# Two attention plans shifted by a few groups, and one weight transfer cut in two, in a kernel bound by TensorE

## The chip, the cores and the metric

One core of one Trainium2 chip. The time is that of one execution on the device, in microseconds; lower is better. A kernel is run several times, and medians are quoted.

## The reference, cut to what matters

```python
k_proj = np.einsum('ks,bhsd->bhkd', E, k)          # 8 batches, 8 heads, 1024 tokens, head size 64
v_proj = np.einsum('ks,bhsd->bhkd', F, v)          # 1024 keys and values become 64
attn   = softmax(scale * q @ k_proj.T)             # 1024 x 64 in each head
x      = (attn @ v_proj) as 8192 tokens x 512
h      = x @ w_in                                  # 512 -> 2048
out    = (h * clip(h + 3, 0, 6) / 6) @ w_out       # 2048 -> 512
```

The attention is small beside the two matrix products that follow it, which are nine tenths of the matmul time.

## The kernel before: the parts that the change and the argument touch

The work goes batch by batch. While the main products of batch b run, the attention of batch b+1 is slipped in between their groups of matmuls, so that ScalarE and VectorE do its exponentials, logarithms and products beside TensorE. There are two kinds of main group: 4 matmuls with w_in (0.86 us), and an output group of 16 matmuls with w_out (3.45 us). Every matmul writes a PSUM tile, which another engine then has to read. The tile of a w_in group is read by a relu on ScalarE and by a product on VectorE (the "relu eviction"), that of an output group by a copy, mostly on ScalarE (the "output copy").

```python
ps_mm = tile_pool(name="ps_mm", bufs=4, space=PSUM)   # tiles of the main groups
ps_at = tile_pool(name="ps_at", bufs=4, space=PSUM)   # tiles of the attention
...
def quads(self, stationary, j):
    tiles = [pat() for _ in range(NB)]                # NB = 2; pat() takes a tile of ps_at
    ...                                               # two matmuls into each
def normalised(self, j):
    den = self.quads(lambda r, h: ones[r:r + KP, :D], j)         # sums of exponentials
    av = self.quads(lambda r, h: self.vp[r:r + KP, h, :], j)     # times the values
    lns = [log(den[t]) for t in range(NB)]                       # ScalarE
    yield
    for t in range(NB):
        nc.vector.tensor_mul(self.xT[:, j, t, :], av[t], inverse(lns[t]))   # ScalarE, then VectorE
        yield
```

A plan is a list of (wait, part, argument): let `wait` places go by, then issue the part. Places lie after each w_in group and after each output group (in batch 1's plan, after each quarter of an output group). "two_scores" makes 16 score matmuls into all four attention tiles; ScalarE reads each tile with an exponential. "project" fills one tile with keys and values, which VectorE copies out in "keys_out" and "values_out". In each plan the four "normalised" steps are called the first to the fourth below, and in the prediction "normalised" 1 to 4; their arguments in the code are 0 to 3. Each gives ScalarE two logarithms and two "reciprocals" (exponentials of the negated logarithm), and VectorE two products. The prediction numbers the groups of a half batch from 0. PSUM tiles are handed out by the framework when the kernel is built, so which tile a matmul gets, and thus what it waits for, can be read from the built program.

The softmax here doesn't subtract the row's maximum and nothing guards it: scores larger than these inputs give would overflow.

## Time and profile before

| | |
|---|---|
| median time | 518.07 us (518.07 to 518.13, 3 runs) |
| span of the profiled run | 516.5 us |
| TensorE busy | 502.4 us, 97% |
| next busiest engine, ScalarE | 282.0 us, 55% |

Where TensorE idles is seen best in the view by windows. The columns are the stretch, its length, TensorE's busy time and instructions, its clock, the busy share of the DMA engines and what they moved:

```profile
0.00:20.00 20.00, 16.94 (x144) 1.00 1.15 180
20.00:36.00 16.00, 15.23 (x81) 1.00 1.29 205
66.00:87.00 21.00, 20.26 (x135) 1.00 1.04 186
104.00:137.00 33.00, 30.95 (x184) 1.00 0.90 152
198.00:460.00 262.00, 259.78 (x1398) 1.00 0.40 86
```

Outside the start and the end, three stretches idle: that of the w_in loads (20 to 36), batch 1's attention (66 to 87) and batch 2's (104 to 137). In the 262 us of the later batches it is under 1%.

### The profile page before, as it was taken

The page shows a single profiled execution, that of the slowest core. Times are in us where ns is not written, and L with a number is a line of the kernel's source. Part 1 is how long each engine was busy: PE and PEld are TensorE (multiplying, and loading weights), DVE is VectorE, ACT ScalarE, POOL GpSimd, SP SyncE. Part 2 cuts the span into 40 slices and gives each one's busy share as a digit, 9 for nine tenths or more (in the row PEclk, how much of TensorE's full clock was granted, in tenths as well). Part 3 has the DMA queues.
Part 4 walks back from the last instruction along what each step waited for, and adds up shares of the span by engine and source line. Part 5 has one row for each costly group of instructions (what it writes and reads, how often), then busy time and mean ns, then how long its engine had stood idle before and what let it go on. Part 6 is the DMA issues. An engine that isn't in the chain of part 4 may idle for free.

```text
span 516.5 us, 7173 instructions
## 1 busy us (share of the span) xinstructions
PE 502.4 (97%) x2752; PEld 222.7 (43%) x2802; DVE 239.4 (46%) x377; ACT 282.0 (55%) x517; POOL 37.2 (7%) x56
## 2 busy tenths in 40 slices
PE   8899999999999999999999999999999999999996
PEld 4444444434344444444444444444444444444442
DVE  3573735744455345445444453544535544344420
ACT  3657466575556743766436753566545674444431
POOL 8510020020020000200010000200000000000000
PEclk9999999999999999999999999999999999999999
DMA  9999999499169511984119820397111011001112
GB/s 169 202 204 208 202 162 209 93 155 212 41 103 214 123 43 30 153 175 102 41 52 188 175 67 34 70 205 151 41 42 39 34 42 41 28 35 43 41 43 80
DMA packets 73683, 55.40 MB, mean 107 GB/s; under 512 B 35504, under 2 KB 65456, under 8 KB 73648
## 3 DMA queue, kind: packets, MB, share of 16 engines
q0 software_dynamic: 31424, 29.36, 36.0%
q1 hardware_dynamic: 42000, 25.17, 18.3%
q8 instruction: 22, 0.36, 0.3%
q10 hardware_dynamic: 224, 0.39, 0.3%
q14 instruction: 13, 0.11, 0.1%
HBM read 59.24 MB, written 16.78 MB: 147 GB/s over the span
## 4 chain that ended last, share of the span: by engine, by line
PE 89%; DMA 3%; ACT 2%; issue 2%; DVE 2%; POOL 1%; another core or an unknown queue 0%; DVEq 0%; ACTq 0%; POOLq 0%
PE mm L421 41%; PE mm L401 41%; PE at L224 3%; PE at L181 3%; DMA w_in_sb<-in_moe_w_in_dram 2%; PE at L210 1%; DMA k<-in_k_dram 1%; DVE g L407 1%; ACT ln L158 0%; ACT r L406 0%; POOL q L97 0%; ACT aT L215 0%; POOL k L101 0%; DVE xT L235 0%
## 5 line engine op out<-in xcount | busy, mean ns | idle before, releaser
L407 DVE SCALAR_TENSOR_TENSOR g<-r,mm 128x512 bf16<-128x512 f32 x256 | 173.2, 685 | 207.0 <-ACT r L406 206.7
L401 PE MATMUL mm<-xT,w_in_sb 128*128 128x512 bf16 x1001 | 232.5, 379 | 3.4 <-issue 1.7
L421 PE MATMUL mm<-w_out_sb,g 128*128 128x512 bf16 x997 | 229.4, 379 | 1.3 <-issue 0.2
L406 ACT ACTIVATE r<-mm 128x512 f32<-128x512 f32 x256 | 152.2, 602 | 67.3 <-PE mm L401 65.6
L401 PEld LDWEIGHTS <-w_in_sb 128*128 128x128 bf16 x1024 | 97.0, 98 | 125.5 <-issue 12.8
L421 PEld LDWEIGHTS <-g 128*128 128x128 bf16 x1024 | 98.9, 98 | 120.6 <-issue 3.8
L435 ACT COPY o_sb<-mm 128x512 f32<-128x512 f32 x59 | 34.3, 586 | 140.0 <-PE mm L421 134.9
L235 DVE TENSOR_TENSOR xT<-at,rec 128x512 bf16<-128x512 f32 x56 | 38.0, 684 | 24.8 <-ACT rec L163 24.8
L163 ACT ACTIVATE rec<-ln 128x512 f32<-128x512 f32 x60 | 37.5, 637 | 0.0
L158 ACT ACTIVATE ln<-at 128x512 f32<-128x512 f32 x60 | 33.0, 615 | 6.2 <-PE at L224 3.9
L215 ACT ACTIVATE aT<-at 128x512 bf16<-128x512 f32 x56 | 29.0, 610 | 2.0 <-PE at L210 2.0
L199 POOL COPY mark<-kT 1x1 bf16<-1x1 bf16 x5 | 0.9, 177 | 246.6 <-DMA kT<-kp 246.6
L224 PE MATMUL at<-aT,vp 64*64 64x512 bf16 x112 | 12.7, 378 | 1.3 <-ACT ln L158 0.8
L181 PE MATMUL at<-k,e_t 128*64 128x512 bf16 x56 | 13.4, 382 | 0.0
L181 PE MATMUL at<-v,f_t 128*64 128x512 bf16 x56 | 13.4, 382 | 0.0
L224 PE MATMUL at<-aT,ones 64*64 64x512 bf16 x112 | 11.5, 400 | 0.1
L210 PE MATMUL at<-qT,kT 64*64 64x256 bf16 x224 | 9.1, 275 | 1.0 <-DVE vp L190 0.9
L190 DVE CAST vp<-at 64x512 bf16<-64x512 f32 x14 | 9.7, 694 | 0.3
L187 DVE CAST kp<-at 64x512 bf16<-64x512 f32 x14 | 8.9, 676 | 1.1 <-PE at L181 1.1
L181 PEld LDWEIGHTS <-e_t 128*64 128x64 bf16 x56 | 5.6, 109 | 7.3 <-issue 3.0
L84 PE MATMUL mm<-ones 128*128 128x512 bf16 x18 | 7.0, 521 | 1.5 <-DVE ones L77 1.5
L224 PEld LDWEIGHTS <-ones 64*64 64x64 bf16 x112 | 3.2, 103 | 11.9 <-issue 11.9
(57 smaller groups left out, 109.0 us busy)
## 6 DMA issues: line engine op xcount, KB each, us to landing
out_dram<-o_sb SPq DMA_DIRECT2D x63, 256.0 KB, 2.0
k<-in_k_dram POOLq DMA_DIRECT2D x7, 1024.0 KB, 14.7
v<-in_v_dram POOLq DMA_DIRECT2D x7, 1024.0 KB, 20.1
q<-in_q_dram POOLq DMA_DIRECT2D x7, 1024.0 KB, 9.8
w_out_sb<-in_moe_w_out_dram POOLq DMA_DIRECT2D x4, 512.0 KB, 18.0
w_in_sb<-in_moe_w_in_dram POOLq DMA_DIRECT2D x3, 512.0 KB, 12.4
k<-in_k_dram POOLq DMA_DIRECT2D x4, 256.0 KB, 5.5
v<-in_v_dram POOLq DMA_DIRECT2D x4, 256.0 KB, 7.7
```

The costliest lines, as they stand in the source:

```text
L158: nc.scalar.activation(ln, den, AF.Ln)
L163: nc.scalar.activation(rec, ln, AF.Exp, scale=-1.0)
L181: nc.tensor.matmul(ps[e * KP:(e + 1) * KP], ef_t[e][:, so, :], kqv[self.b]["kv"[e]][:, :, so, :], start=(so == 0), stop=(so == SO - 1))
L210: nc.tensor.matmul(tiles[r][t * KP:(t + 1) * KP, a * HT:(a + 1) * HT], self.kT[r * D:(r + 1) * D, 2 * j + a, :], qT[r * D:(r + 1) * D, j, ...
L215: nc.scalar.activation(self.aT[j][:, r].rearrange("p a n -> p (a n)"), tiles[r], AF.Exp, scale=scale)
L224: nc.tensor.matmul(tiles[t][c:c + D].rearrange("p (r n) -> p r n", r=2), stationary(r, 2 * j + a), self.aT[j][r:r + KP, :, a, :], start=Tr ...
L235: nc.vector.tensor_mul(self.xT[:, j, t, :], av[t], inverse(lns[t]))
L401: nc.tensor.matmul(h_ps, w_in_sb[:, ko, fo * P:(fo + 1) * P], xT[:, ko, t, :], start=(ko == 0), stop=(ko == KO - 1))
L406: nc.scalar.activation(r, h_ps, AF.Relu, bias=0.5, scale=1.0 / 6.0)
L407: nc.vector.scalar_tensor_tensor(g[:, fo, :], r, 1.0, h_ps, op0=ALU.min, op1=ALU.mult)
L421: nc.tensor.matmul(o_ps, g[:, fo, c * P:(c + 1) * P], w_out_sb[:, fo, :], start=(fo == 0), stop=(fo == FO - 1))
L435: (copy or nc.scalar.copy)(o_sb, o_ps)
```

## The change

Its intent: let the first groups start on w_in sooner, and move the attention steps of batches 1 and 2 to places where what they wait for is ready.

```diff
-    for lo, n in ((0, 128), (128, 128), (256, 256), (512, 512), (1024, 512), (1536, 512)):
+    for lo, n in ((0, 128), (128, 128), (256, 256), (512, 256), (768, 256),
+                  (1024, 512), (1536, 512)):
         load_w_in(lo, n)
 ...
     PLANS = {1: (... (2, "values_out", 1),
-                 (1, "two_scores", 0), (3, "two_scores", 2), (1, "normalised", 0),
+                 (1, "two_scores", 0), (2, "two_scores", 2), (2, "normalised", 0),
                  (0, "normalised", 1), (0, "normalised", 2), (0, "normalised", 3)),
              2: ((10, "project"), (0, "keys_out"), (1, "turn"), (2, "values_out", 0), (3, "values_out", 1),
-                 (1, "two_scores", 0), (2, "two_scores", 2), (3, "normalised", 0),
-                 (0, "normalised", 1), (1, "normalised", 2), (0, "normalised", 3))}
+                 (3, "two_scores", 0), (1, "two_scores", 2), (4, "normalised", 0),
+                 (0, "normalised", 1), (0, "normalised", 2), (0, "normalised", 3))}
```

## The prediction

> **What bounds the kernel now.** I read the page of the profile first, for the share of each engine and the chain that ended last; then TensorE's timeline, for every place where it stops; then the timelines of ScalarE and VectorE around those places, to see what TensorE was waiting for.
>
> ```profile
> span 516.5 us, 7173 instructions
> PE 502.4 (97%) x2752; PEld 222.7 (43%) x2802; DVE 239.4 (46%) x377; ACT 282.0 (55%) x517; POOL 37.2 (7%) x56
> ...
> PE 89%; DMA 3%; ACT 2%; issue 2%; DVE 2%; POOL 1%; another core or an unknown queue 0%; DVEq 0%; ACTq 0%; POOLq 0%
> ```
>
> TensorE is the bound: 97% busy, and 89% of the chain is its own matmuls; the next engine is at 55%. The change adds and removes no TensorE instruction (2752 matmuls stand in both), it only moves some. So all it can do is shorten or lengthen the places where TensorE stops, and 516.5 - 502.4 = 14.1 us is the whole idle time, of which the table of windows puts 3.1 into the first 20 us and 4.4 into the last 56.5. The prize is a few tenths of a per cent. I list the stops that the change can reach.
>
> First, the wait for w_in. The columns 512 to 1023 come in one transfer, and the fifth group needs its first 128 columns:
>
> ```profile
> 24.60 9.67 PE L401 MATMUL mm<-xT,w_in_sb 128*128 128x512 bf16 x43 [0.35 <-DMA w_in_sb<-in_moe_w_in_dram]
> ```
>
> Second, batch 1. "normalised" is 4 matmuls with ones and 4 with vp; run freely (77.25 to 77.81) it takes 0.56 us. At 73.18 it takes until 74.79, so 1.61:
>
> ```profile
> 71.65 0.63 PE L210 MATMUL at<-qT,kT 64*64 64x256 bf16 x16
> 72.22 1.04 PE L421 MATMUL mm<-w_out_sb,g 128*128 128x512 bf16 x4
> 73.18 0.47 PE L224 MATMUL at<-aT,ones 64*64 64x512 bf16 x4
> 73.73 0.89 PE L224 MATMUL at<-aT,vp 64*64 64x512 bf16 x4
> 74.79 2.54 PE L421 MATMUL mm<-w_out_sb,g 128*128 128x512 bf16 x11 [0.16 <-issue]
> 77.25 0.41 PE L224 MATMUL at<-aT,ones 64*64 64x512 bf16 x4
> 77.50 0.39 PE L224 MATMUL at<-aT,vp 64*64 64x512 bf16 x4
> 77.81 2.76 PE L421 MATMUL mm<-w_out_sb,g 128*128 128x512 bf16 x12
> ```
>
> ```profile
> 72.11 2.07 ACT L215 ACTIVATE aT<-at 128x512 bf16<-128x512 f32 x4 [1.19 <-PE at L210]
> ```
>
> The attention has four PSUM tiles. The scores just before fill all four, and each is free only when its exponential has read it: ScalarE does that until 74.18, and the last two matmuls with vp need the fourth. The idle mark shows little of this (0.16), since a stretched group counts as busy; the start of the following row shows it. The loss is 1.61 - 0.56 = 1.05 us.
>
> Third, batch 2, with three stops:
>
> ```profile
> 104.25 0.51 PE L210 MATMUL at<-qT,kT 64*64 64x256 bf16 x9
> 105.64 0.41 PE L210 MATMUL at<-qT,kT 64*64 64x256 bf16 x7 [0.88 <-DVE vp L190]
> 105.98 1.90 PE L401 MATMUL mm<-xT,w_in_sb 128*128 128x512 bf16 x8
> ...
> 123.62 0.41 PE L224 MATMUL at<-aT,ones 64*64 64x512 bf16 x4
> 123.86 0.85 PE L224 MATMUL at<-aT,vp 64*64 64x512 bf16 x4
> 124.64 3.63 PE L421 MATMUL mm<-w_out_sb,g 128*128 128x512 bf16 x16
> ...
> 129.92 0.41 PE L224 MATMUL at<-aT,ones 64*64 64x512 bf16 x4
> 130.19 0.40 PE L224 MATMUL at<-aT,vp 64*64 64x512 bf16 x2
> 131.44 0.40 PE L224 MATMUL at<-aT,vp 64*64 64x512 bf16 x2 [0.85 <-ACT ln L158]
> 131.78 1.90 PE L401 MATMUL mm<-xT,w_in_sb 128*128 128x512 bf16 x8
> ```
>
> ```profile
> 104.89 0.69 DVE L190 CAST vp<-at 64x512 bf16<-64x512 f32 x1
> ```
>
> The scores stop in their tenth matmul, which takes the tile that "project" filled: VectorE copies vp out of it until 105.58. 105.98 - 104.25 = 1.73 where 16 such matmuls take 0.56: 1.17 us lost. The third "normalised" (123.62) loses 1.02 - 0.56 = 0.46, the fourth (129.92) 1.86 - 0.56 = 1.30. Together 2.93 us.
>
> **What the Trainium skill says.** "PSUM — Partial Sum Buffer", section The four PSUM rules: one matmul output is at most one bank, 512 fp32 values; Specifications (TRN2) gives 8 banks. The kernel has 4 tiles of 128x512 f32 for the main matmuls and 4 for the attention, so no fifth attention tile is to be had; the stops above agree. "Perfetto Trace Analysis", section Identifying the Most-Contended Engine, warns that matmul busy time is no measure of headroom, since pipelined matmuls overlap; the trace agrees (379 ns each, yet 16 take 3.45 us, 0.216 apiece), so I count by starts. The same page, section DMA Optimizations, says that splitting a transfer may let some work start sooner, and that small ones cost throughput. "DMA: Bandwidth & Descriptors", section Specifications, wants at least 512 B for line rate; a 256-column piece writes rows of just 512 B. The trace has one such piece: it landed 1.31 us after the piece before it, a 512-column one 2.55 us after. So halves cost 2 x 1.31 - 2.55 = 0.07 us more.
>
> **The change, part by part.**
>
> *w_in.* The pieces landed at 22.01 (columns to 511), 24.56, 27.10 and 29.68. With 256 more columns alone, the first half lands at 22.01 + 1.31 = 23.32; TensorE wants it at 24.60 - 0.35 = 24.25. The wait goes. The second half, at 24.63, is wanted two groups later (24.25 + 2 x 0.863 = 25.98). The next piece lands at 27.17 and is now wanted at 24.25 + 4 x 0.863 = 27.70: it holds, by 0.5 us. Later ones have more: the second q half landed at 32.30 and is wanted at 33.8, w_out's first piece at 34.84 for 35.5, v of batch 1 at 53.45 for 54.9, qT at 66.62 for 68.0. All else up to there follows TensorE. Gain 0.35 us.
>
> *Batch 1.* The second scores move 4 matmuls (0.86 us) earlier, "normalised" stays. The first scores began at 68.40 and their exponentials ended at 70.91; the second scores now begin at 68.40 + 0.56 + 8 x 0.216 = 70.7 and need the fourth tile only at about 71.0, so they just don't wait. Their exponentials begin 0.46 later, 71.2, and end at 73.2. "normalised" starts at 73.15 as before, but its fourth tile is wanted at 73.15 + 0.37 = 73.5: free. Gain 1.05 us. Following: the second "normalised" then comes 1.05 earlier (76.2) and needs the products of the first: logarithms from 73.5, reciprocals from 74.45, products 75.15 to 76.45 by the pitch of this trace, wanted at 76.57. It fits, by 0.1 us, so I count 1.0.
>
> *Batch 2.* The order of the changed program: first scores two groups later, second scores one output group (16 matmuls) after them, "normalised" 1 to 4 after groups 7, 9, 11 and 14 of the second half, where they were after groups 5, 7, 11 and 13.
> - First scores: at 104.15 + 2 x 0.863 = 105.87, after vp's copy (105.58). Gain 1.17.
> - Second scores: 4 us after the first; their exponentials are done by 112.7, "normalised" 1 comes at 113.9. No stop, though four relu evictions queue behind the exponentials.
> - "normalised" 2: now stands where 4 stood, two groups after an output group. Its last two matmuls have been given the tile of its own first denominator, so they wait for its own logarithm, and before that ScalarE has, in order, the output copy, a reciprocal, a relu, a reciprocal, a relu: the very sequence of 128.30 to 131.4 before. New loss 1.30.
> - "normalised" 3: after an output group of 3.45 us. Loss 0 in place of 0.46.
> - "normalised" 4: three groups after 3, with six ScalarE instructions and its own logarithm ahead of its last tile. From the end of the output group: copy at 0.15, then pitches of about 0.5: logarithms 0.65 and 1.15, relu 1.7, reciprocal 2.2, relu 2.7, reciprocal 3.2, relu 3.7, logarithm 4.2 to 4.8; its matmuls end at 5.15, freely at 0.56 + 2.59 + 0.56 = 3.71. Loss 1.45 in place of 1.30.
> Sum: 1.30 + 1.45 = 2.75 against 2.93. Gain 0.18 us: the stops move rather than go.
>
> In all 0.35 + 1.0 + 0.18 = 1.53 us, so 518.07 - 1.5 = 516.5. Batches 3 to 7 keep their plan.
>
> **Rivals.** (1) Batch 2 gains in full: its author meant to move the stops away. If 2 and 4 did not wait, 2.7 us more would go, 513.8. Against it stands the order of ScalarE's instructions, known from the changed program. (2) Batch 2 gets worse: the second scores after an output group put the exponentials ahead of four relu evictions, the main tiles come free late, and the output group waits. By my working the tile it needs is free at 113.95 and wanted at 114.45; if ScalarE is half a microsecond later, some tenths are lost, and the time is 517 to 517.5. (3) The loads bind: earlier TensorE work waits for the piece at 27.17 or for q, and the 0.35 is given back: 516.9. The landing times leave 0.5 us at the tightest. (4) Batch 1 only hands its stop on, to the products before "normalised" 2: up to 0.3 us back, 516.8.
>
> **Range and chances.** The two sure terms are 1.4 us; batch 2 is worth -0.2 with an error of some 0.6 either way. Rivals 2 to 4 pull up, 1 far down but unlikely: 515.7 to 517.3. Two per cent is 10.4 us, nearly all the idle time there is, so faster and slower by that much get 1% each.
>
> **What would show it.** In the changed trace: no wait for w_in at the fifth group; in batch 1 the first "normalised" in 0.56 us; in batch 2 all 16 first score matmuls in one row, a stop of about 1.3 us in the last two matmuls of "normalised" 2 marked with the logarithm, none at 3, about 1.45 at 4; batches 3 to 7 61.2 us apart as now. It is wrong if "normalised" 2 or 4 run freely, or if a main group waits for VectorE near the second output group.

## The result, and the profile after

The changed kernel took 516.7 us (median of 4 runs, 516.49 to 516.83); the kernel before, in the same rounds, 518.1 us (518.07 to 518.32). The ratio is 0.9972, with a 95% interval of 0.9954 to 0.9989. Ratios here are the mean time of one kernel's fast runs over that of the other's of the same rounds, so not quite the ratio of the medians. In the profile the span fell from 516.5 to 515.0 us; the engines' shares and TensorE's share of the chain:

```profile
span 515.0 us, 7174 instructions
PE 501.9 (97%) x2752; PEld 223.0 (43%) x2802; DVE 239.1 (46%) x377; ACT 281.9 (55%) x517; POOL 37.9 (7%) x57
...
PE 93%; DMA 3%; issue 2%; ACT 1%; POOL 1%; DVE 0%; ACTq 0%; DVEq 0%; POOLq 0%
```

The one instruction more is the added transfer, on POOL. Now TensorE's timeline of the changed kernel (start, length, engine, line, operation, operands, count, and in brackets the idle time before with its releaser). The lines are numbered one higher than before, because the diff adds one. First, w_in:

```profile
20.52 0.38 PE L402 MATMUL mm<-xT,w_in_sb 128*128 128x512 bf16 x1 [0.54 <-DMA w_in_sb<-in_moe_w_in_dram]
20.82 0.40 PE L322 MATMUL at<-aT,vp 64*64 64x512 bf16 x2
21.16 12.74 PE L402 MATMUL mm<-xT,w_in_sb 128*128 128x512 bf16 x57
33.74 0.61 PE L302 MATMUL at<-ident,q 128*128 128x128 bf16 x8
```

The w_in groups run in one row from 21.16 to 33.74, with no stop in them. Then batch 1's first "normalised" step, with the row after it:

```profile
72.81 0.41 PE L225 MATMUL at<-aT,ones 64*64 64x512 bf16 x4
73.05 0.39 PE L225 MATMUL at<-aT,vp 64*64 64x512 bf16 x4
73.59 2.54 PE L422 MATMUL mm<-w_out_sb,g 128*128 128x512 bf16 x11 [0.16 <-issue]
76.06 0.41 PE L225 MATMUL at<-aT,ones 64*64 64x512 bf16 x4
```

The matmuls with vp follow those with ones at once, in 0.39 us in place of 0.89. The row after them says x11 where the program has 12 matmuls: the record of the first is missing, it started some 0.22 us before 73.59, and the step was free. One stop of batch 1 stays: its fourth step takes 1.16 us (82.57 to 83.73) where the kernel before took 1.15 (83.77 to 84.92), 0.6 more than freely, and is marked with VectorE's product. It stands at this size in every kernel here. Last, batch 2, first scores and the second, third and fourth "normalised" steps:

```profile
104.78 0.63 PE L211 MATMUL at<-qT,kT 64*64 64x256 bf16 x16
105.34 3.63 PE L422 MATMUL mm<-w_out_sb,g 128*128 128x512 bf16 x16
...
118.86 0.41 PE L225 MATMUL at<-aT,ones 64*64 64x512 bf16 x4
119.14 0.40 PE L225 MATMUL at<-aT,vp 64*64 64x512 bf16 x2
120.39 0.40 PE L225 MATMUL at<-aT,vp 64*64 64x512 bf16 x2 [0.85 <-ACT ln L159]
120.95 1.67 PE L402 MATMUL mm<-xT,w_in_sb 128*128 128x512 bf16 x7 [0.16 <-issue]
...
126.01 0.41 PE L225 MATMUL at<-aT,ones 64*64 64x512 bf16 x4
126.25 0.39 PE L225 MATMUL at<-aT,vp 64*64 64x512 bf16 x4
126.57 2.76 PE L402 MATMUL mm<-xT,w_in_sb 128*128 128x512 bf16 x12
129.26 0.41 PE L225 MATMUL at<-aT,ones 64*64 64x512 bf16 x4
129.61 0.40 PE L225 MATMUL at<-aT,vp 64*64 64x512 bf16 x2
130.79 0.40 PE L225 MATMUL at<-aT,vp 64*64 64x512 bf16 x2 [0.77 <-ACT ln L159]
131.35 0.81 PE L402 MATMUL mm<-xT,w_in_sb 128*128 128x512 bf16 x3 [0.16 <-issue]
```

The scores run in one row. The second and the fourth step stop before their last two matmuls, and the third runs in 0.56 us. The rows after the second and the fourth lack their first record too (x7 of 8, x3 of 4), so 0.22 us is to be taken off: each step takes 2.09 - 0.22 = 1.87 us, a loss of 1.31.

Where the time came from is seen by setting five starts side by side:

| TensorE reaches | before, us | after, us | gained so far |
|---|---|---|---|
| first w_out matmul | 35.87 | 35.49 | 0.38 |
| batch 1, first scores | 68.40 | 68.02 | 0.38 |
| batch 1, second "normalised" | 77.25 | 76.06 | 1.19 |
| batch 2, first w_in group after its last "normalised" and output group | 136.97 | 135.45 | 1.52 |
| end of the span | 516.5 | 515.0 | 1.5 |

So w_in gave 0.38 us, batch 1 0.81 and batch 2 0.33, and nothing came or went later.

### The profile page after: what moved, and what is told of

Same layout as the page of the kernel before. It is cut to its first block, busy times and chain, and to the rows that moved or that the text cites. A ratio compares the mean times of both kernels' runs of the same rounds, so it can differ in the third digit from the quotient of the medians.

```text
span 515.0 us, 7174 instructions
## 1 busy us (share of the span) xinstructions
PE 501.9 (97%) x2752; PEld 223.0 (43%) x2802; DVE 239.1 (46%) x377; ACT 281.9 (55%) x517; POOL 37.9 (7%) x57
## 4 chain that ended last, share of the span: by engine, by line
PE 93%; DMA 3%; issue 2%; ACT 1%; POOL 1%; DVE 0%; ACTq 0%; DVEq 0%; POOLq 0%
PE mm L402 43%; PE mm L422 42%; PE at L225 3%; PE at L182 3%; DMA w_in_sb<-in_moe_w_in_dram 2%; PE at L211 2%; DMA k<-in_k_dram 1%; ACT ln L159 0%; ACT rec L164 0%; PE at L322 0%; POOL q L97 0%; POOL k L101 0%; PE at L302 0%; DVE g L408 0%; DVE o_sb L436 0%
```

## The experiments

The theory: each gain is a wait of TensorE that ends earlier, the wait being for the landing of a piece (w_in) or for one of the four PSUM tiles of the attention (batches 1 and 2); the three add up. The rivals: gains are handed on to a later wait; or it is not the tile but ScalarE's and VectorE's results that are late, and the stop returns elsewhere. All kernels gave correct results. The runs came on two chips; the kernel before took 518.37 us (518.15 to 518.60, 9 runs) in the first and 518.13 us (518.00 to 519.00, 9 runs) in the second. The changed kernel was not run again: "the changed kernel" below is the 516.7 us of its own rounds, in which the kernel before took 518.1, as in the second.

| run | what | median, us | before | ratio, 95% interval |
|---|---|---|---|---|
| e1_w_in | w_in alone | 517.72 | 518.37 | 0.9993, 0.9980 to 1.0005 |
| e2_batch1 | plan of batch 1 alone | 517.32 | 518.37 | 0.9983, 0.9970 to 0.9995 |
| e3_batch2 | plan of batch 2 alone | 517.87 | 518.37 | 0.9993, 0.9980 to 1.0005 |
| e5_tile_batch1 | before, one borrowed tile | 517.62 | 518.37 | 0.9988, 0.9973 to 1.0003 |
| e4_replan2 | changed, another plan of batch 2 | 515.41 | 518.13 | 0.9946, 0.9933 to 0.9958 |
| e6_tile_batch2 | changed, two borrowed tiles | 514.20 | 518.13 | 0.9922, 0.9908 to 0.9935 |
| e7_both2 | e4's plan, one borrowed tile | 514.30 | 518.13 | 0.9926, 0.9913 to 0.9938 |
| e8_w_in_late | changed, a larger w_in piece | 517.97 | 518.13 | 0.9996, 0.9980 to 1.0010 |

Effects of a few tenths of a microsecond are within these intervals (e1, e3, e5); for those the rows of the trace decide: the same stop in two runs agrees to some 0.02 us once the loads are past.

### One part of the change at a time

**e1_w_in**: the first hunk of the diff alone.

> The kernel before with the w_in pieces split alone. Theory (the stop at the fifth group ends when columns 512 to 639 land, and half a piece lands 1.3 us after the piece before it): no wait for w_in at the fifth group, everything after it 0.35 to 0.4 us earlier, batches 1 and 2 as before (losses 0.83 and 2.93 us): 517.7 us. Rival (the gain is handed back to a later load or to the smaller transfers): the first w_out matmuls start at 35.87 as before, or a later group waits for a piece, 518.1 us.

As the theory has it: no stop between the w_in groups. The median was 517.72 us. The profiled run itself was an outlier at 518.63 us: its last piece of v landed at 19.72 us (18.45 in the changed kernel's profile), and TensorE began its long row 0.7 us later; from the start of the long w_in row to the next kind of matmul it took 34.45 - 21.87 = 12.58 us, as in the changed kernel (33.74 - 21.16), and the kernel before 34.11 - 21.01 = 13.10.

**e2_batch1**: the plan of batch 1 alone. Its rows, none of which lacks a record:

> The kernel before with the plan of batch 1 alone. Theory (the first normalised waited for the tile that the fourth exponential of the scores just before had not read yet): that normalised takes 0.56 us in place of 1.39 (counting the first matmul of the next row, whose record is missing), the rest as before: 0.83 us off, 517.3 us. Rival (the stop is handed on to the second normalised or to the first group of batch 1): less than 0.5 us off, with a new stop at the second normalised.

```profile
73.21 0.41 PE L224 MATMUL at<-aT,ones 64*64 64x512 bf16 x4
73.45 0.39 PE L224 MATMUL at<-aT,vp 64*64 64x512 bf16 x4
73.76 2.76 PE L421 MATMUL mm<-w_out_sb,g 128*128 128x512 bf16 x12
76.46 0.41 PE L224 MATMUL at<-aT,ones 64*64 64x512 bf16 x4
76.70 0.39 PE L224 MATMUL at<-aT,vp 64*64 64x512 bf16 x4
77.02 2.76 PE L421 MATMUL mm<-w_out_sb,g 128*128 128x512 bf16 x12
```

The steps take 0.55 and 0.56 us; nothing was handed on. The second started 76.46 - 68.42 = 8.04 us after the first scores, where the kernel before took 77.25 - 68.40 = 8.85: 0.81 us gained.

**e3_batch2**: the plan of batch 2 alone.

> The kernel before with the plan of batch 2 alone. Theory (the stops move: first scores 1.17 to 0, second scores and first normalised 0, normalised 2 from 0 to 1.31, 3 from 0.46 to 0, 4 stays 1.31): 2.93 lost becomes 2.62, 0.3 us off, 517.8 us. Rival (batch 2 is where the change gains, the other parts are small): 1 us or more off, 517.1 us or less.

The stops moved as expected: scores free at 106.15, the second step from 120.23 to 122.09 (1.86 us), the third free, the fourth from 130.63 to 132.49 (1.86 us). The rival, a gain of 1 us or more, falls. The parts of the three runs, by their ratios, are 0.36, 0.88 and 0.36 us of 518, 1.6 us together; the whole change gave 1.4 by its medians. Within the spread they add up. By the rows the stops shrank by 0.52 (e1), 0.81 (e2) and 0.33 us (e3, 2.93 - 2 x 1.30), 1.66 together; the profile of the whole change gained 1.52, having begun its long w_in row 0.15 later.

### Is it the tile?

**e5_tile_batch1**: the kernel before, with its plans and pieces, but for batch 1's first "normalised" step the last tile comes from the main pool:

```diff
-        def quads(self, stationary, j):
-            tiles = [pat() for _ in range(NB)]
+        def quads(self, stationary, j, last=pat):
+            tiles = [pat(), last()]
 ...
-            av = self.quads(lambda r, h: self.vp[r:r + KP, h, :], j)
+            spare = pmm if (self.b, j) == (1, 0) else pat
+            av = self.quads(lambda r, h: self.vp[r:r + KP, h, :], j, spare)
```

> The kernel before, plans and pieces untouched, but the fourth tile of batch 1's first normalised comes from the main matmuls' tiles, one of which is idle there. Theory (a PSUM tile is what is waited for): its last two matmuls no longer wait for the fourth exponential; only the third matmul pair still waits for the third exponential, so the loss falls from 0.83 to about 0.3 us, 517.6 us. Rival (ScalarE's results or TensorE's own switch from one kind of matmul to the other make the stop): the loss stays 0.8 us, 518.1 us.

```profile
73.01 0.47 PE L224 MATMUL at<-aT,ones 64*64 64x512 bf16 x4
73.56 0.40 PE L224 MATMUL at<-aT,vp 64*64 64x512 bf16 x2
73.57 0.40 PE L224 MATMUL mm<-aT,vp 64*64 64x512 bf16 x2
73.91 2.76 PE L422 MATMUL mm<-w_out_sb,g 128*128 128x512 bf16 x12
```

The two matmuls that write the borrowed tile ("mm") start with the pair before them. The step takes 73.91 - 73.01 = 0.90 us, a loss of 0.34 in place of 0.83, with all else at its place (the later stops keep their 1.16, 1.73, 1.02 and 1.86 us): the fourth tile was what the kernel before waited for. What is left fits the third tile's wait for the third exponential, in size and in place (the pair with vp starts 0.55 us after the first matmul in place of 0.24); no run tests it apart.

**e6_tile_batch2**: the changed kernel with the same edit for `(self.b, j) in ((2, 1), (2, 3))`, the second and the fourth step of batch 2.

> The changed kernel, same plans, but the last tile of normalised 2 and 4 of batch 2 comes from the main matmuls' four tiles. Theory (only the tile is missing): both stops of 1.31 us go, no main group waits long, 2.6 us less than the changed kernel, 514.1 us. Rival (ScalarE and VectorE are simply late there; a tile taken from the main groups makes those wait instead): the stop comes back before a main group within 5 us, less than 1 us gained, 515.7 us or more.

```profile
118.98 0.41 PE L225 MATMUL at<-aT,ones 64*64 64x512 bf16 x4
119.26 0.40 PE L225 MATMUL at<-aT,vp 64*64 64x512 bf16 x2
119.26 0.40 PE L225 MATMUL mm<-aT,vp 64*64 64x512 bf16 x2
119.60 1.90 PE L403 MATMUL mm<-xT,w_in_sb 128*128 128x512 bf16 x7
...
128.13 0.41 PE L225 MATMUL at<-aT,ones 64*64 64x512 bf16 x4
128.49 0.40 PE L225 MATMUL at<-aT,vp 64*64 64x512 bf16 x2
128.49 0.40 PE L225 MATMUL mm<-aT,vp 64*64 64x512 bf16 x2
129.06 0.81 PE L403 MATMUL mm<-xT,w_in_sb 128*128 128x512 bf16 x3 [0.16 <-issue]
```

Both stops are gone but for 0.06 us at the second step (0.62 us) and 0.15 at the fourth (0.71, with 0.22 taken off for the missing first record of the row after it). The main groups, now with a tile less for a while, don't wait: the fourth step's end to the first w_in group of the next batch takes 133.16 - 129.06 = 4.10 us, as in the changed kernel (135.45 - 131.35). 514.20 us, 2.5 less than the changed kernel's 516.7. The rival falls: the wait was for a tile, not for results of ScalarE or VectorE.

### Is it the place?

**e4_replan2**: the changed kernel with batch 2's plan rearranged:

```diff
-              2: (... (2, "values_out", 0), (3, "values_out", 1),
-                 (3, "two_scores", 0), (1, "two_scores", 2), (4, "normalised", 0),
-                 (0, "normalised", 1), (0, "normalised", 2), (0, "normalised", 3))}
+              2: (... (2, "values_out", 0), (1, "values_out", 1),
+                 (3, "two_scores", 0), (2, "two_scores", 2), (3, "normalised", 0),
+                 (0, "normalised", 1), (2, "normalised", 2), (0, "normalised", 3))}
```

> The changed kernel with another plan of batch 2: vp's second copy one group earlier, first scores back to where they were, normalised 2 straight after an output group (as 1 group of 16 w_out matmuls gives ScalarE 3.45 us), 3 straight after the next, 4 as in the changed kernel. Theory (the place decides, by what ScalarE and VectorE have to do since the last one): first scores free, normalised 1, 2 and 3 free, 4 still 1.31 lost: 1.31 us less than the changed kernel, 515.4 us. Rival (the stops only move round, two of them always remain): within 0.3 us of the changed kernel, 516.7 us.

```profile
102.97 0.63 PE L211 MATMUL at<-qT,kT 64*64 64x256 bf16 x16
103.54 1.90 PE L402 MATMUL mm<-xT,w_in_sb 128*128 128x512 bf16 x8
...
124.72 0.41 PE L225 MATMUL at<-aT,ones 64*64 64x512 bf16 x4
124.96 0.39 PE L225 MATMUL at<-aT,vp 64*64 64x512 bf16 x4
125.28 2.76 PE L402 MATMUL mm<-xT,w_in_sb 128*128 128x512 bf16 x11
127.98 0.41 PE L225 MATMUL at<-aT,ones 64*64 64x512 bf16 x4
128.33 0.40 PE L225 MATMUL at<-aT,vp 64*64 64x512 bf16 x2
129.50 0.40 PE L225 MATMUL at<-aT,vp 64*64 64x512 bf16 x2 [0.77 <-ACT ln L159]
```

The first scores stand where they stood before the change and run freely, with vp's copy moved ahead by two places of the plan (two groups; the expectation says one). Beside the plan before the change, this one moves only that copy, and the third and fourth steps by one place back. Of the four steps only the last stops. 515.41 us, 1.3 less than the changed kernel. So the two stops of the changed plan were not bound to remain.

**e7_both2**: e4's plan with one borrowed tile, for the fourth step.

> The plan of e4_replan2 with the borrowed tile for normalised 4 alone. Theory: all stops of batch 2 gone, 2.6 us less than the changed kernel, 514.1 us, the same as with two borrowed tiles. Rival as there: 515.4 us or more.

514.30 us, the same as e6 within their spread (514.26 to 514.60 against 514.06 to 514.51). Two different ways reach the same time once batch 2 has no stop left.

### Is it the landing?

**e8_w_in_late**: the changed kernel with w_in cut differently.

```diff
-    for lo, n in ((0, 128), (128, 128), (256, 256), (512, 256), (768, 256),
-                  (1024, 512), (1536, 512)):
+    for lo, n in ((0, 128), (128, 128), (256, 256), (512, 256), (768, 768),
+                  (1536, 512)):
```

> The changed kernel with the pieces of w_in after column 768 cut the other way (768 to 1535 in one, then 1536 on). Theory (a group waits until the whole piece that holds its columns has landed, at 2.55 us per 512 columns): the piece lands at 23.5 + 3.85 = 27.35, wanted at 26.1 by the seventh group: a stop of about 1.2 us there, and 1.2 us slower than the changed kernel, 517.9 us. Rival (fewer, larger transfers make up for it, or a later stop absorbs it): within 0.4 us of the changed kernel.

```profile
21.05 4.97 PE L402 MATMUL mm<-xT,w_in_sb 128*128 128x512 bf16 x22
27.09 7.94 PE L402 MATMUL mm<-xT,w_in_sb 128*128 128x512 bf16 x35 [1.08 <-DMA w_in_sb<-in_moe_w_in_dram]
```

The 768-column piece landed at 27.05 by the trace, and TensorE went on at 27.09, after six groups. 517.97 us, 1.3 more than the changed kernel: a group waits for the whole piece that holds its columns, and a wait there is not absorbed later.

## Why the prediction was right, point by point

**The bound and the size of the prize.** Right: no instruction of TensorE was added or removed, and the whole effect is in places where it stops. 516.5 us was predicted, 516.7 measured. That the sum is so close is luck in part: batch 1 was 0.19 us over and batch 2 0.15 under. The 2752 matmuls that the prediction names are records; the program has 2802. So the 14.1 us of idle time hold missing records too: the profile of e2, which has all records, shows 515.7 - 505.7 = 10.0 us.

**w_in, 0.35 us.** Right in size, but for a reason that hides two errors of opposite sign. The stop was read from the idle mark (0.35). By starts it was larger: 13.10 us against 12.58 for the same matmuls, so 0.52. The mark is short because the profile models the end of a matmul at 379 ns while the next may start 216 ns after it: 163 ns of each wait do not show. So the group wanted its columns at 24.09, not at 24.25. The wait also varies with the landings: in the three other profiles with the whole piece (e2, e3, e5) it is 0.34 to 0.42 us by starts, where the marks say 0.18 to 0.25. On the other side, in the changed kernel's profiled run the first piece of w_in landed at 20.24 in place of 20.10, and TensorE began its long row 0.15 later. That this is no effect of the change is likely, since the very first load of that run, ahead of all changed lines, was late already (6.63 in place of 6.55), and over the ten profiles the first piece landed from 19.87 to 20.37 us without the split and from 20.06 to 20.41 with it. The landing of the halves was predicted at 23.32 and 24.63, and was 23.50 and 24.84; the next piece came at 27.41 where 27.17 was predicted, and its group started at 27.69, so its margin was 0.3 us and not the 0.5 that were claimed, but it held.

**Batch 1, 1.0 us.** The mechanism was right (e2, e5), the term was mis-sized: it measured 0.81. The step that failed is "The loss is 1.61 - 0.56 = 1.05 us", read from the start of the row at 74.79. That row has x11 where the program has 12 matmuls; its first record is missing, and the true start was 0.22 us earlier. The count stood in the line that was quoted, and 2752 beside 2802 on the page. The idle mark of 0.16 us that the prediction explains ("a stretched group counts as busy") is no wait either: it is the hole of that missing record. Of the wait itself two gaps of 0.09 us are left, which the view does not mark; the rest lies under the records of the matmuls. The 0.05 us that were held back for the second step's products were not needed.

**Batch 2, 0.18 us.** Right in mechanism, 0.33 measured. That the stops would move from the scores, the third and the fourth step to the second and the fourth was read from the tiles given out in the built program, and came as said. The second step was predicted to lose 1.30 us and lost 1.31. The fourth was predicted at 1.45 and lost 1.31: the working by pitches left out that each switch from main matmuls to attention matmuls costs TensorE some 0.1 us (8 w_in matmuls take 1.83 us ahead of such a switch, 1.73 without), so the step arrived 0.1 us later (3.25 us after the output group, not 3.15) and waited that much less, which is most of the difference.

**The rivals.** Rival 1 (batch 2 gains in full) was excluded by e3. e6 and e7 show the time it would have made, 514.2 to 514.3, where the prediction said 513.8. Rival 2 (main groups wait near the second output group) did not occur: the four relu activations behind the exponentials ran one behind the other (111.41 to 113.73), the w_in groups did not wait, and the output group followed the first "normalised" step at once (113.58). Rivals 3 and 4 did not occur either; e8 shows that rival 3 was real as a mechanism, since a piece that lands 1 us late costs just that. One thing that the prediction closed off was open: "no fifth attention tile is to be had" holds for the eight banks, but e5, e6 and e7 took one from the main groups, which did not miss it.

## What to carry to other kernels

Where one engine is 97% busy, list its stops by the starts of its rows, and check the count of each row against the program before you subtract. When a step stops on a tile that is read by another engine, moving it helps only if that engine has got through its queue by then, not if the same queue stands before the new place: here the new plan of batch 2 turned 2.93 us of stops into 2.62. A tile borrowed from a pool that had one to spare removed nearly all of both stops at once.

## What the Trainium skill lacked or had wrong

- "TensorE: Matmul & The Clock Gate", section Back-to-back issue gap, gives about 131 ns per matmul of 512 columns as the sustained pace of a stream of weight loads and matmuls, and calls its 216 ns only the isolated gap. Here 16 matmuls, each with a weight load of its own, take 3.45 us, 216 ns apiece, at a granted clock of 1.0, and no row of these matmuls shown here is faster.
- "TensorEngine Tiling (Array Packing)", section Key Properties, says that changing the tiling mode drains TensorE, without a figure. In these runs the switch from 128x128 matmuls to the 64x64 ones of the attention costs some 0.1 us (1.83 us for 8 matmuls in place of 1.73).
- "Perfetto Trace Analysis", section Identifying the Most-Contended Engine, warns against matmul busy time because pipelined instructions look smaller in the trace. Here they hardly do: a record of 512 columns lasts 379 ns in a row, at a pitch of 216, and 389 as the first after a wait. Nor is it said that the idle gaps of TensorE come out short by the difference: a wait of 0.52 us by starts showed as 0.35. The page does not warn of missing records either: 50 of 2802 matmuls have none in six of the ten profiles, and all have one in the other four.
- "DMA: Bandwidth & Descriptors", section Specifications, asks for at least 512 B, which reads as if halving a piece down to that were free. Pieces with rows of just 512 B landed 1.34 us apart, two of them in 2.68 us against 2.55 for one of twice the width: 5% more. The 768-column piece of e8 landed 3.75 us after the one before it (23.30 to 27.05), so the three widths fit some 0.13 us for each piece and 1.2 us for each 256 columns. Whether the 0.13 us belong to the transfer or to its rows, 512 in each piece, no run here tells.
